# The gate logits as one more column of a projection's weights, in a fused linear-attention kernel

## The chip, the cores and the metric

The kernel runs on one core of one Trainium2 chip. The metric is the device time of one execution in microseconds (us). The kernel before took 189.98 us (median of 3 runs, 189.82 to 190.57).

## The reference

Two linear-attention blocks, A and B, read the same x (2048 rows of 640, bf16), and a gate mixes their outputs:

```
g = sigmoid((x * gate_w).sum(-1))                 # one number per row
block(x, wqkv, wo):                               # 32 heads of 20
    q, k, v = x @ wqkv, by heads
    phi(t) = where(t > 0, t + 1, exp(t)) + 1e-6
    kv = phi(k)^T v;  z = sum of phi(k) over the rows      # per head
    o = (phi(q) kv) / (phi(q) z + 1e-6)
    return o @ wo
out = g * block_A + (1 - g) * block_B
```

## The kernel before, in words

The five engines are TensorE (PE: matmuls, with PEld its weight loads), VectorE (DVE), ScalarE (ACT), GpSimd (POOL) and SyncE (SP, which issues most loads and stores). The order of nearly all work is written out by hand in the program; each engine runs its own instructions in that order and waits where an input isn't ready. PE's results go to PSUM, in four slots of two banks that are used in rotation (`ps`, lines 74 to 81): a slot can be written again when its last reader is done.

x is held twice: `xn` has rows on the partitions (16 chunks of 128 rows), `xT` is transposed (5 column blocks of 128 by 2048 rows). The first four chunks are transposed by PE (`x_transpose`, line 207, a DVE copy out of PSUM at line 214), the other twelve by transposing loads (line 155).

The start (lines 137 to 155): x arrives in four pieces and the k weights of A, `wk[0]`, in five column blocks, on the queues of SP and ACT in turn: SP has x 0, weights 0, weights 2, weights 3 and 4; ACT has x 1, weights 1, x 2, x 3. Then SP issues the q weights of A (line 151) and the fifteen transposing loads. `k_first` (line 265) does the first four chunks of k: transposes of chunks 0 and 1, their matmuls on column blocks 0 and 1, the transpose of chunk 2, and so on, as the pieces arrive. A chunk of k is 10 matmuls (5 column blocks by two halves `hf` of 320 columns; `k_mm`, line 249), and then phi (class `Phi`): ACT takes the exponential `e` (line 225), DVE clamps it (`clamp`, line 230) and takes the larger of it and t + 1 (`top`, line 239) into `pk`.

Then come, for A, the chunks 4 to 15 of k and the first five units of q. `q_pass` (line 743) has the other five q units (`q_unit`: 10 matmuls of 512 columns, and phi), and between the first and the second of them the gate pass and `z_rows` (line 510, the sum of `pk` over the rows, `zA`, which DVE brings to `zr`). `x_sum`, `k_sum` and `sq_sum` are sums on DVE for products done with seven instead of eight multiplications (Strassen); `g_strassen` (line 458) is such a product. In it, `rec_pass` (line 573) computes the denominators of A, `denA`, on PE; DVE multiplies them by a gate factor and takes the reciprocal.

The gate pass (`gate_pass`, line 198): the gate weights came by a load of 640 single elements (line 776, `gcol`), are widened to 32 equal columns by DVE (line 791, `gwr`), and PE multiplies them with `xT` in 40 matmuls (`by_group`, line 188) into `lg`. All 32 partitions of a group hold the same logits, in the layout of the denominators: partition 32 j + h, column for a row of x. ACT takes exp(-logit) and exp(logit) (line 204, `geA` and `geB`), DVE adds 1 (line 205). The denominators of A are multiplied by 1 + exp(-logit) = 1/g, those of B by 1 + exp(logit) = 1/(1 - g), so that the normalization does the gating too (line 582).

After that come the k and q of B in one interleaved stage, its `g` product, the folding of v and wo into one matrix for each block (`M`; for A it goes through `m_rows` in DRAM), and the output products with seven multiplications for a pair of chunks (lines 907 on), each stored by SP.

Of the kernel before, what the change touches and what calls it, by code (L numbers as in the profile page):

```python
# [8 lines left out]
P = 128  # L9
FP32 = mybir.dt.float32  # L10
BF16 = mybir.dt.bfloat16
ACT = mybir.ActivationFunctionType
# [4 lines left out]
DT = D // P  # L17
# [3 lines left out]
HB = 512  # L21
# [11 lines left out]
def kernel(  # L33
# [47 lines left out]
    def ps(name, slot=None):  # L81

        return ps_raw(name, slot).bitcast(FP32).rearrange("p (b n) -> p b n", b=2)
# [16 lines left out]
    ones = persist.tile([P, H], BF16, name="ones")  # L100
    gwr = persist.tile([P, DT, H], BF16, name="gwr")
    hc, ic = ST // 2, 2 * P
# [18 lines left out]
    )]  # L121
    ge = [persist.tile([P, 2 * RB], FP32, name=f"ge{b}") for b in "AB"]

# [10 lines left out]
    wq = [None, None]  # L134
    wk[0] = wpool.tile([P, DT, D], BF16, tag="wk", name="wkA")
    def load_x(eng, lo, hi):
        eng.dma_start(out=xn[:, lo:hi, :], in_=xb0[:, lo:hi, :])

    def load_wk(eng, lo, hi):
        eng.dma_start(out=wk[0][:, lo:hi, :], in_=wq_dram[0][:, lo:hi, D:2 * D])  # L140

# [3 lines left out]
    load_wk(nc.scalar, 1, 2)  # L145
    load_wk(nc.sync, 2, 3)
    load_x(nc.scalar, 2, 3)
    load_wk(nc.sync, 3, DT)
    load_x(nc.scalar, 3, 4)
    wq[0] = wpool.tile([P, DT, D], BF16, tag="wq", name="wqA")  # L150
    nc.sync.dma_start(out=wq[0][:], in_=wq_dram[0][:, :, 0:D])
    gcol = persist.tile([P, DT], BF16, name="gcol")
    for n in range(1, NB):
# [27 lines left out]


    warm = ps("warm", 3)
    one_l, one_r = [nc.const_aps.tensor(1.0, [P, n], BF16) for n in (P, HB)]
# [12 lines left out]

    def gate_pass():

        pt = ps("lg")  # L200
        for h in range(2):
            by_group(pt[:, 0, h * RB:(h + 1) * RB], gwr, xT, h)
        for b in range(2):
            nc.scalar.activation(out=ge[b][:], in_=pt[:, 0, :], func=ACT.Exp, scale=(-1.0, 1.0)[b])
            nc.vector.tensor_scalar(ge[b][:], ge[b][:], 1.0, 1e30, op0=ALU.add, op1=ALU.min)

    def x_transpose(i, slot, eng, cuts=(0, DT)):
        pt = ps_raw("xt", slot)
        for c in range(DT):
            nc.tensor.transpose(out=pt[:, c * P:(c + 1) * P], in_=xn[:, i, c * P:(c + 1) * P], identity=ident[:])  # L210
        copy = nc.scalar.copy if eng == "act" else nc.vector.tensor_copy
        src = pt[:, 0:D].rearrange("p (c n) -> p c n", c=DT)
        for lo, hi in zip(cuts, cuts[1:]):
            copy(out=xT[:, lo:hi, i * P:(i + 1) * P], in_=src[:, lo:hi])

    class Phi:
# [31 lines left out]

    def k_mm(b, i, c, pt, hf):
        nc.tensor.matmul(  # L250
            pt[:, hf, 0:HF], lhsT=xT[:, c, i * P:(i + 1) * P], rhs=wk[b][:, c, hf * HF:(hf + 1) * HF],
            start=(c == 0), stop=(c == DT - 1),
        )

    def k_done(b, i, pt):
        phi(pk[:, i, :].rearrange("p (b n) -> p b n", b=2), pt[:, :, 0:HF])

# [7 lines left out]
    def k_first():  # L265

        pts = [ps("kA", (2 + i) % 4) for i in (0, 1)]

        def part(i, cs):
            for c in cs:  # L270
                for hf in range(2):
                    k_mm(0, i, c, pts[i], hf)

        for i in range(2):
            x_transpose(i, i, "dve", (0, 2, DT))
        for i in range(2):
            part(i, (0, 1))
        x_transpose(2, 0, "dve", (0, 2, DT))
        for i in range(2):
            part(i, (2,))  # L280
        pts.append(ps("kA", 1))
        part(2, (0, 1, 2))
        x_transpose(3, 0, "dve")
        for i in range(3):
            part(i, (3, 4))
            k_done(0, i, pts[i])
        k_chunk(0, 3, 0)

# [284 lines left out]
    def rec_pass(b, zsel, slot):  # L573
# [5 lines left out]
        for h in range(2):  # L579
            part = slice(h * RB, (h + 1) * RB)  # L580
            d1 = work.tile([P, RB], FP32, tag="d1", name="d1")
            nc.vector.scalar_tensor_tensor(
                out=d1[:], in0=pt[:, 0, part], scalar=EPS, in1=ge[b][:, part], op0=ALU.add, op1=ALU.mult
            )
# [158 lines left out]
    def q_pass(units):  # L743

        units = list(units)
        q_unit(0, *units.pop(0))
        gate_pass()
        zr = z_rows(0)
        for k in range(2):
            x_sum(1 + k)  # L750
            q_unit(0, *units.pop(0), True)
# [10 lines left out]
    with tc.manual_schedule():  # L762
# [8 lines left out]
        for i in range(hc, ST - 2):  # L771
            k_chunk(0, i)
            if i == hc:
                sq_sum(4, 0)
    with nc.allow_non_contiguous_dma(reason="640 elements, one to a partition and column"):
        nc.sync.dma_start(out=gcol[:], in_=gate_w.rearrange("(c p) -> p c", p=P))
    for n in range(1, NB):
# [4 lines left out]
    load_wo(0, nc.sync)  # L782
    wk[1] = load_w(1, "k", nc.sync)

# [3 lines left out]
    with tc.manual_schedule():  # L788
        k_chunk(0, ST - 2)
        turn[0] = (turn[0] + 1) % 4  # L790
        nc.vector.tensor_copy(out=gwr[:], in_=gcol[:, :, None].to_broadcast([P, DT, H]))
        k_chunk(0, ST - 1)
        k_sum(0, 1)
        zsel = q_pass([(m, 1) for m in range(DT)])
# [69 lines left out]

        scratch = ctx.enter_context(tc.tile_pool(name="scratch", bufs=1, space=bass.MemoryType.DRAM))
        m_rows = scratch.tile([D, D], BF16, name="m_rows")

# [144 lines left out]
```

## Time and profile before

| | |
|---|---|
| median of 3 runs | 189.98 us |
| the profiled execution's own time | 191.16 us |
| its span (first to last instruction) | 189.4 us |
| PE busy | 184.4 us (97%) |
| DVE busy | 156.0 us (82%) |
| ACT busy | 86.7 us (46%) |
| read from and written to HBM | 10.00 and 3.44 MB |

The busy time of PE counts an instruction from its start to its end, and matmuls overlap, so the distance from one matmul's start to the next one's tells more. "Chain" is the work that ended last, followed back from the last instruction: at each step to what released it. "Landing" is the time from a load's issue to the signal that it is complete. A group of a line is written as: line, engine, operation, output <- inputs, shape.

### The profile page before, as it was taken

To read this page: it belongs to the slowest core of one execution; us is meant where nothing else is said; L and a number is where in the kernel's file an instruction comes from. 1 tells how busy PE (TensorE), PEld (TensorE's weight loads), DVE (VectorE), ACT (ScalarE), POOL (GpSimd) and SP (SyncE) were. 2 spreads that over 40 slices of the span, in tenths; PEclk is the share of its full clock that TensorE was granted. 3 is DMA by queue.
4 is the path that set the end of the run, shared out by engine and by line. 5 is a ranking of instruction groups with operands and counts; after the bars stand their busy time and mean duration, and the time that the engine had idled before them with its cause. 6 is when DMAs were issued, how large, how long until landed. Compare 5 with 4: busy or idle time off the path is not lost.

```text
span 189.4 us, 3688 instructions
## 1 busy us (share of the span) xinstructions
PE 184.4 (97%) x1494; PEld 123.6 (65%) x1494; DVE 156.0 (82%) x267; ACT 86.7 (46%) x134; POOL 8.6 (5%) x23
## 2 busy tenths in 40 slices
PE   8899999999999999999999999999999999999992
PEld 3566657766567677676666665767677776777771
DVE  1368968999898999998898987999997989787553
ACT  2055478544963351563959685662611611111110
POOL 8900000000000000000000000000000000000000
PEclk9999999999999999999999999999999999999999
DMA  6984439992040000005000000146600003213112
GB/s 181 321 147 88 105 61 315 324 194 106 3 143 31 3 0 0 0 3 165 8 3 2 0 0 0 29 137 214 146 0 3 0 3 108 99 39 106 69 69 71
DMA packets 19759, 15.64 MB, mean 83 GB/s; under 512 B 9502, under 2 KB 19614, under 8 KB 19742
## 3 DMA queue, kind: packets, MB, share of 16 engines
q1 hardware_dynamic: 18878, 14.59, 28.0%
q10 hardware_dynamic: 864, 0.82, 1.3%
q8 instruction: 11, 0.18, 0.4%
q14 instruction: 6, 0.05, 0.1%
HBM read 10.00 MB, written 3.44 MB: 71 GB/s over the span
## 4 chain that ended last, share of the span: by engine, by line
PE 91%; DMA 3%; DVE 2%; ACT 1%; ACTq 0%; issue 0%; DVEq 0%
PE gs L453 16%; PE qA L294 11%; PE kA L250 11%; PE kB L250 11%; PE q L348 7%; PE ox L653 6%; PE oy L653 5%; PE oz L653 5%; DMA xn<-in_A_x_dram 3%; PE ow L653 3%; PE gB L424 2%; PE gA L424 2%; PE qB L294 1%; PE q L294 1%; DVE osb L658 1%; PE mA L872 1%
## 5 line engine op out<-in xcount | busy, mean ns | idle before, releaser
L250 PEld LDWEIGHTS <-xT 128*128 128x128 bf16 x320 | 31.4, 99 | 15.0 <-issue 0.2
L230 DVE TENSOR_SCALAR e<-e 128x640 bf16<-128x640 bf16 (+2 forms) x56 | 19.3, 344 | 6.9 <-ACT e L225 6.7
L250 PE MATMUL kB<-wkB,xT 128*128 128x320 bf16 x160 | 24.2, 299 | 0.0
L250 PE MATMUL kA<-wkA,xT 128*128 128x320 bf16 x160 | 23.4, 306 | 0.0
L294 PE MATMUL qA<-xT,wqA 128*128 128x512 bf16 x100 | 22.4, 379 | 0.0
L294 PEld LDWEIGHTS <-wqA 128*128 128x128 bf16 x100 | 11.6, 118 | 9.3 <-issue 0.3
L225 ACT ACTIVATE e<-kA 128x640 bf16<-128x640 f32 x16 | 11.1, 704 | 13.3 <-PE kA L250 13.2
L453 PEld LDWEIGHTS <-xn 128*128 128x128 bf16 x128 | 12.2, 98 | 5.2 <-issue 0.5
L225 ACT ACTIVATE e<-kB 128x640 bf16<-128x640 f32 x16 | 11.3, 708 | 9.0 <-PE kB L250 8.9
L239 DVE SCALAR_TENSOR_TENSOR pk<-kA,e 128x640 bf16<-128x640 f32 x16 | 13.2, 824 | 1.7
L239 DVE SCALAR_TENSOR_TENSOR pk<-kB,e 128x640 bf16<-128x640 f32 x16 | 13.2, 823 | 1.5
L225 ACT ACTIVATE e<-qA 128x1024 bf16<-128x1024 f32 x10 | 10.2, 1024 | 8.6 <-PE qA L294 8.1
L697 ACT COPY u<-ox 128x320 f32<-128x320 f32 x8 | 3.4, 426 | 21.9 <-PE ox L653 21.9
L225 ACT ACTIVATE e<-q 128x512 bf16<-128x512 f32 x18 | 10.8, 598 | 5.4 <-PE q L348 3.8
L653 PEld LDWEIGHTS <-xT 128*128 128x128 bf16 x85 | 8.0, 98 | 3.0 <-DVE xT L592 0.2
L653 PEld LDWEIGHTS <-pqTA 128*128 128x128 bf16 x85 | 7.9, 98 | 2.9 <-issue 0.2
L653 PEld LDWEIGHTS <-pqTB 128*128 128x128 bf16 x80 | 7.8, 98 | 3.0
L453 PE MATMUL gs<-pk,xn 128*128 128x320 bf16 x64 | 9.5, 299 | 0.0
L348 PE MATMUL q<-xT,wqB 128*128 128x512 bf16 x32 | 9.5, 379 | 0.0
L658 DVE TENSOR_TENSOR osb<-oz,u 128x320 bf16<-128x320 f32 (+1 forms) x18 | 8.0, 452 | 1.6 <-PE oz L653 0.9
L424 PEld LDWEIGHTS <-xn 128*128 128x128 bf16 x64 | 6.3, 98 | 3.0 <-issue 0.4
L681 ACT COPY p1s<-ox 128x320 f32<-128x320 f32 x8 | 3.4, 426 | 10.0 <-PE ox L653 10.0
(145 smaller groups left out, 319.5 us busy)
## 6 DMA issues: line engine op xcount, KB each, us to landing
out_dram<-osb SPq DMA_DIRECT2D x14, 160.0 KB, 1.8
xn<-in_A_x_dram SPq DMA_DIRECT2D x3, 640.0 KB, 6.7
wqA<-in_A_wqkv_dram SPq DMA_DIRECT2D x1, 800.0 KB, 6.6
wvA<-in_A_wqkv_dram SPq DMA_DIRECT2D x1, 800.0 KB, 10.3
wkB<-in_B_wqkv_dram SPq DMA_DIRECT2D x1, 800.0 KB
wqB<-in_B_wqkv_dram SPq DMA_DIRECT2D x1, 800.0 KB, 4.5
wvB<-in_B_wqkv_dram SPq DMA_DIRECT2D x1, 800.0 KB, 4.5
MA<-m_rows SPq DMA_DIRECT2D x1, 800.0 KB, 4.5
```

The lines of the kernel that those rows point to most:

```text
L225: nc.scalar.activation(out=to, in_=part, func=ACT.Exp)
L230: nc.vector.tensor_scalar(self.e, self.e, 1.0, EPS, op0=ALU.min, op1=ALU.add)
L239: nc.vector.scalar_tensor_tensor(out=dst, in0=src, scalar=1.0 + EPS, in1=e, op0=ALU.add, op1=ALU.max)
L250: nc.tensor.matmul(pt[:, hf, 0:HF], lhsT=xT[:, c, i * P:(i + 1) * P], rhs=wk[b][:, c, hf * HF:(hf + 1) * HF], start=(c == 0), stop=(c == D ...
L294: nc.tensor.matmul(dst, lhsT=mixed(wq[b][:, c, :], m), rhs=xT[:, c, n * HB:(n + 1) * HB], start=first, stop=last,)
L348: nc.tensor.matmul(dst, lhsT=left(c), rhs=right(c), start=first and k == 0, stop=k == len(cs) - 1, skip_group_check=not first,)
L424: nc.tensor.matmul(pt[:, hf, 0:HF], lhsT=xn[:, i, c * P:(c + 1) * P], rhs=pk[:, i, hf * HF:(hf + 1) * HF], start=(i == 0), stop=(i == ST - 1),
L453: nc.tensor.matmul(pt[:, n, 0:HF], lhsT=left[:, i, n * P:(n + 1) * P], rhs=right[:, i, :], start=(first and i == 0), stop=(i == hc - 1), s ...
L653: nc.tensor.matmul(dst, lhsT=left[:, c, r0:r0 + P], rhs=right[:, c, :], start=(first and c == 0), stop=(c == DT - 1), skip_group_check=not ...
L658: nc.vector.tensor_tensor(out=dst, in0=acc, in1=sb, op=ALU.add)
L681: nc.scalar.copy(out=self.p1s[:], in_=self.at("x"))
L697: nc.scalar.copy(out=self.u2[:], in_=self.at("x"))
```

## The change

The gate logits are no longer a pass of their own. The gate weights become column 640 of the tile of A's k weights, so that the second half of each `kA` matmul has 321 columns and the logit of every row comes out in PSUM column 320 of that half, with rows on the partitions. ACT takes its exponential by chunk (`gl`, one column each); after the last chunk DVE makes both factors from it (`gate_rows`: a clamp, a reciprocal, an added 1). `gate_spread` brings them into the layout of the denominators: one transpose on PE (fp32, with an fp32 identity that POOL makes, held in the not yet used `GT[0]`), a copy by ACT, a store of 32 rows to DRAM (`g_rows`), and four loads that broadcast them over 32 partitions each into `ge`.

The column itself comes from a load of the gate weights as 5 rows of 128 (`g5`), transposed by PE and copied by DVE (`gate_column`), early in `k_first`. There the order is now: transposes of chunks 0 and 1, first halves of chunk 0 (two matmuls), `gate_column`, first halves of chunk 1, second halves of both, column block 2 of both, transposes of chunks 2 and 3, then the rest. Each `x_transpose` is copied by DVE (blocks 0 and 1) and ACT (blocks 2 to 4). The loads: SP has x 0, weights 0, gate weights, x 2 and 3 in one; ACT has x 1, weights 1, weights 2, weights 3 and 4. The load of B's k weights is issued a little later in program order.

```diff
-    wk[0] = wpool.tile([P, DT, D], BF16, tag="wk", name="wkA")
+    wk[0] = wpool.tile([P, DT, D + 2], BF16, tag="wk", name="wkA")
...
     load_x(nc.sync, 0, 1)
     load_x(nc.scalar, 1, 2)
     load_wk(nc.sync, 0, 1)
     load_wk(nc.scalar, 1, 2)
-    load_wk(nc.sync, 2, 3)
-    load_x(nc.scalar, 2, 3)
-    load_wk(nc.sync, 3, DT)
-    load_x(nc.scalar, 3, 4)
+    nc.sync.dma_start(out=g5[:], in_=gate_w.rearrange("(c p) -> c p", p=P))
+    load_wk(nc.scalar, 2, 3)
+    load_x(nc.sync, 2, 4)
+    load_wk(nc.scalar, 3, DT)
...
-    def gate_pass():
-        pt = ps("lg")
-        for h in range(2):
-            by_group(pt[:, 0, h * RB:(h + 1) * RB], gwr, xT, h)
-        for b in range(2):
-            nc.scalar.activation(out=ge[b][:], in_=pt[:, 0, :], func=ACT.Exp, scale=(-1.0, 1.0)[b])
-            nc.vector.tensor_scalar(ge[b][:], ge[b][:], 1.0, 1e30, op0=ALU.add, op1=ALU.min)
+    def gate_column(pt):
+        nc.tensor.transpose(out=pt[:, 2 * HB:2 * HB + DT], in_=g5[:], identity=ident[0:DT, 0:DT])
+        nc.vector.tensor_copy(out=wk[0][:, :, D:D + 1], in_=pt[:, 2 * HB:2 * HB + DT, None])
+    def gate_rows():
+        nc.vector.tensor_scalar(gf[:, 1], gl[:], 1e-30, 1e30, op0=ALU.max, op1=ALU.min)
+        nc.vector.reciprocal(out=gf[:, 0], in_=gf[:, 1])
+        nc.vector.tensor_scalar(gf[:], gf[:], 1.0, 1e30, op0=ALU.add, op1=ALU.min)
+    def gate_spread():
+        pt = ps("gt")
+        nc.tensor.transpose(out=pt[0:2 * ST, 0, 0:P], in_=gf[:].rearrange("p b i -> p (b i)"), identity=ident32)
+        rows = work.tile([2 * ST, P], FP32, tag="d1", name="gr")
+        nc.scalar.copy(out=rows[:], in_=pt[0:2 * ST, 0, 0:P])
+        nc.sync.dma_start(out=g_rows[:], in_=rows[:])
+        by_group = g_rows[:].rearrange("(g j r) p -> j g (r p)", g=4, j=4)
+        for j in range(4):
+            nc.sync.dma_start(
+                out=ge[32 * j:32 * j + 32].rearrange("p b (h n) -> p (b h) n", h=2),
+                in_=by_group[j][None].to_broadcast([H, 4, RB]),
+            )
...
     def k_mm(b, i, c, pt, hf):
+        n = HF + (b == 0 and hf == 1)
         nc.tensor.matmul(
-            pt[:, hf, 0:HF], lhsT=xT[:, c, i * P:(i + 1) * P], rhs=wk[b][:, c, hf * HF:(hf + 1) * HF],
+            pt[:, hf, 0:n], lhsT=xT[:, c, i * P:(i + 1) * P], rhs=wk[b][:, c, hf * HF:hf * HF + n],
...
     def k_done(b, i, pt):
-        phi(pk[:, i, :].rearrange("p (b n) -> p b n", b=2), pt[:, :, 0:HF])
+        f = Phi(pk[:, i, :].rearrange("p (b n) -> p b n", b=2), pt[:, :, 0:HF])
+        if b == 0:
+            nc.scalar.activation(out=gl[:, i:i + 1], in_=pt[:, 1, HF:HF + 1], func=ACT.Exp)
+        f.clamp()
+        f.top()
...
-        for i in range(2):
-            x_transpose(i, i, "dve", (0, 2, DT))
-        for i in range(2):
-            part(i, (0, 1))
-        x_transpose(2, 0, "dve", (0, 2, DT))
+        pt = [x_transpose(i, i) for i in range(2)]
+        part(0, (0, 1), (0,))
+        gate_column(pt[0])
+        part(1, (0, 1), (0,))
+        for i in range(2):
+            part(i, (0, 1), (1,))
         for i in range(2):
             part(i, (2,))
-        pts.append(ps("kA", 1))
+        for i in (2, 3):
+            x_transpose(i, i - 2)
+        pts.append(ps("kA", 0))
         part(2, (0, 1, 2))
-        x_transpose(3, 0, "dve")
         for i in range(3):
             part(i, (3, 4))
             k_done(0, i, pts[i])
-        k_chunk(0, 3, 0)
+        k_chunk(0, 3, 1)
...
         q_unit(0, *units.pop(0))
-        gate_pass()
         zr = z_rows(0)
+        gate_spread()
...
-    wk[1] = load_w(1, "k", nc.sync)
...
-        nc.vector.tensor_copy(out=gwr[:], in_=gcol[:, :, None].to_broadcast([P, DT, H]))
         k_chunk(0, ST - 1)
+        gate_rows()
+        wk[1] = load_w(1, "k", nc.sync)
```

## The prediction

> **What bounds the kernel now.** I read the busy times first, then the chain of work that ended last in order of time, then the instructions in order of time for the two stretches that the change touches. The page's first line:
>
> ```profile
> PE 184.4 (97%) x1494; PEld 123.6 (65%) x1494; DVE 156.0 (82%) x267; ACT 86.7 (46%) x134; POOL 8.6 (5%) x23
> ```
>
> TensorE (PE) has almost no idle time. The chain (start, length, what) says where it has some, and what the gate costs:
>
> ```profile
> 1.73 5.91 DMA xn<-in_A_x_dram
> 7.64 0.05 issue
> 7.69 0.45 PE xt L210 x5
> ...
> 39.87 2.16 PE qA L294 x10
> 42.03 1.21 PE lg L193 x39
> 43.24 1.09 PE zA L516 x32
> 44.32 4.45 PE qA L294 x20
> ```
>
> To 7.64 us a load of x is waited for; from there to 115 us the chain is PE work with no gap. PE's time there counts in full, and the gate logits (`lg`) stand in the chain with 1.21 us. The only other gap is 3.4 us around 115 to 118.4, where PE waits for the last results of its own work; it moves with PE. What could keep PE from using a gain is VectorE (DVE), so I read its instructions around the gate pass:
>
> ```profile
> 41.11 0.82 DVE L239 SCALAR_TENSOR_TENSOR pk<-kA,e 128x640 bf16<-128x640 f32 x1
> 41.85 1.48 DVE L592 TENSOR_TENSOR pqTB<-pk 128x2560 bf16<-128x2560 bf16 x1
> 43.25 0.42 DVE L230 TENSOR_SCALAR e<-e 128x1024 bf16<-128x1024 bf16 x1
> 43.77 1.23 DVE L239 SCALAR_TENSOR_TENSOR pqTA<-qA,e 128x1024 bf16<-128x1024 f32 x1
> 44.91 0.42 DVE L205 TENSOR_SCALAR geA<-geA 128x512 f32<-128x512 f32 x1
> 45.24 0.42 DVE L205 TENSOR_SCALAR geB<-geB 128x512 f32<-128x512 f32 x1
> 45.58 0.82 DVE L521 TENSOR_TENSOR zr<-zA,E 128x640 bf16<-128x640 f32 x1
> ...
> 59.95 0.69 DVE L325 TENSOR_TENSOR SQ<-xT,SQ 128x1024 bf16<-128x1024 bf16 x1
> 61.06 0.42 DVE L582 SCALAR_TENSOR_TENSOR d<-denA,geA 128x256 f32<-128x256 f32 x1 [0.42 <-PE denA L193]
> ```
>
> DVE runs nearly without a pause, but its last step here (line 582) still waits 0.42 us for PE. In the stretch 45.6 to 65.4 the table by stretches gives DVE 18.20 busy of 19.80 us. So it has 1.6 us to give, if it isn't itself made late.
>
> **The change, part by part.**
>
> *Gate pass out of PE:* -1.21 us (the chain's row). The first `q` unit's matmuls end at 42.03; `zA` then starts there instead of at 43.24. Its first matmuls read old chunks of `pk`, and the last chunk is written at 41.11 + 0.82 = 41.93, so nothing is late.
>
> *The logits' new place:* 80 matmuls of `kA` with 321 columns for 320. Matmuls of 320 columns start 0.136 us apart and of 512 columns 0.216, so a column is 0.4 ns: 80 x 0.4 ns = +0.03 us. Every width in this trace is even; what an odd one does isn't shown. The bounds are nothing and the pitch that the same matmuls have before 6.85 us, 0.267 us, which would be +10.5 us; I take the slope, to which all rows keep.
>
> *16 small Exp on ACT:* ACT takes 704 ns for 640 columns and 1024 ns for 1024, so about 0.17 us with one column, 2.7 us in all. ACT idles 0.65 us ahead of nearly each `e` of the `kA` chunks; that covers it. DVE's step waits for `e`, which comes first. Without the cover it would be 0.17 us a chunk.
>
> *Transpose of the factors on PE, fp32, behind `zA`:* bf16 transposes of x start 0.056 us apart. The trace has no fp32 one: at least 0.06 us, at most four times that for the load of the weights and the pass (0.099 us is a weight load of 128 columns), 0.06 x 4 + 0.1 = 0.36 us. I take +0.2 us, the middle. It doesn't wait: its input is ready near 42.6 us, PE is there at 43.1.
>
> *DVE at the gate:* two steps of line 205 go (44.91 to 45.58, 0.67 us) and the copy into `gwr` (0.31 us, in time where DVE would wait for `e` anyway). Three dependent small steps come in ahead of the `k_sum` at 41.85. A TENSOR_SCALAR takes 320 ns for 640 columns and 424 for 1024, so 0.15 us for none; RECIPROCAL takes 1753 ns for 256 columns, so 0.11 us more for 16; dependent steps stand 0.1 us apart (43.67 to 43.77). That is about 0.68 us. Bounds: 3 x 0.06 (the smallest MEMSET, 59 ns) = 0.2, and 2.2 us if the reciprocal's time were fixed. So `zr` starts where it did, while what lies between is 0.68 us later. That matters once: the third `q` unit of this pass writes the PSUM slot of the first, which DVE frees at 45.00, then at 45.68. PE would be there at 42.03 + 1.09 + 0.2 + 2.17 = 45.49. So PE may wait 0.2 us; with the low bound not at all. I take +0.1 us. From `zr` on DVE has 14.3 us of work to the end of line 325's sums, so it is done near 60.0; `denA` would end near 60.1. Line 582 still waits for PE, and the gain goes through to the rest.
>
> *Store by rows, four broadcast loads:* SP is idle here (it waits 12.9 us for `qA` before it issues `wqB` at 53.31). A store to `m_rows` lands after 2.0 us, 800 KB from there after 4.5; with five issues of 0.4 us the factors are in place near 52.5 us, and line 582 reads them at 60. Free; if not, `rec_pass` would wait. The later issue of `wkB`, the missing `gcol` load (0.58 us of SP at 25.67) and a second identity on POOL, which is done at 9.9 us, are free in the same way.
>
> *The start.* Before, the third piece of x (third on ACT's queue) landed at 7.64, and 32 matmuls and 10 transposes behind it led to the first `qA` matmul at 12.62. On SP's queue the third load landed at 1.71 + 4.4 = 6.11; the trace's completion signals put the fourth ones at 8.57 (SP, 800 KB then through) and 8.79 (ACT, 640 KB). PE is slow there too: `kA` matmuls start 0.267 us apart until 6.85 and 0.136 after. Now both late pieces of x are one load in SP's fourth place, and the weights' third piece and last two pieces are third and fourth on ACT. Four things can be last:
> - PE itself: twelve matmuls and one small transpose from 5.01 on (eight slow, four fast) end near 7.5; then 10 transposes x 0.056, of which the first five, a copy and its signals take 0.83 (as from 7.69 to 8.525 before), and 28 matmuls x 0.136 = 3.81: 7.5 + 0.83 + 3.81 = 12.2.
> - x: 640 KB of SP's queue, halfway between 6.11 and 8.57: 7.34, and + 4.64 = 12.0.
> - weights 2: between 6.11 and 7.64 (the third places); four matmuls more, + 5.18: 11.3 to 12.8.
> - weights 3 and 4: 800 KB on ACT's queue: between 8.79 and 8.79 + 1.15 (the step from 7.64 to 8.79 once more) = 9.94; 22 matmuls follow, + 2.99: 11.8 to 12.9.
>
> So the first `qA` comes between 12.2 and 12.9. The last item, in its middle, gives 12.35; I take 12.4, **-0.2 us**, bounds -0.4 and +0.3. The gate column's own load is 1.2 KB; if it landed as late as the third SP load (6.11), PE would lose 0.6 us of its slack and come to 12.8, inside the bounds.
>
> The Trainium skill (DMA: Bandwidth & Descriptors, Rules for kernel authors) says that spreading loads over the issuing engines brings no bandwidth, since all queues run on the same 16 DMA engines and interleave. The trace agrees so far that both queues' last loads landed 0.2 us apart. By it the bytes would land as before, the last at 8.79, the start would be PE's 12.2, and the sum 0.2 us lower; an estimate.
>
> **Sum:** -1.21 + 0.03 + 0.2 + 0.1 - 0.2 = **-1.08 us**. The profiled execution took 191.16 us (span 189.4), which makes 190.08; the median of the runs shown is 189.98, 1.18 below the profiled one, and the difference taken from it gives **188.9 us** (-0.57%). A measurement tells about 0.5%, 0.95 us, from no change: 189.03 and 190.93 are the borders.
>
> **Rivals.**
> - *DVE becomes the bound at the gate.* The three small steps delay the PSUM slot. With the upper bound of 2.2 us the slot is free at 47.2, PE waits 1.7 us, and the sum is -1.08 - 0.1 + 1.7 = +0.5: 190.5; with 1.5 us it is 189.8. For it: DVE has no pause from 41.1 to 46.3. Against: RECIPROCAL has 256 columns in its row, here it has 16. Chance 0.10.
> - *The start is late.* ACT's last weights share the DMA engines with `wqA`, which SP issues at 4.06 and which landed at 10.66. If they land only then, the first `qA` is at 13.65, +1.03: -0.88 + 1.03 = +0.15, 190.1. For it: ACT's third load landed 1.5 us behind SP's third. Chance 0.13.
> - *Slower: the column waits for all weights.* The gate column is written into the tile that the weight loads still fill. If DVE's copy has to wait for the last of them (8.8 to 9.9), then eight matmuls (1.1), ten transposes and their copy (0.83 from the first) and 28 matmuls (3.81) stand behind it: 14.5 to 15.6, +1.9 to +3.0, less 0.88: about 191.5. It decides from a column at 7.8 us on. For it: PE stands in order behind that copy. Against: line 214 copied into `xT` at 4.67 while loads into other columns of `xT` were under way from 4.48 on. Chance 0.09.
> - *Odd widths.* From 14 ns a matmul on (80 x 14 ns = 1.1 us) nothing of the gain is left; 26 ns (2.1 us) gives 190.9, and the slow pitch of 0.267 us some 199. Nothing in the trace speaks for it. Chance 0.08.
>
> **How the numbers follow.** Forecast 0.60, from 188.5 (all low ends: -1.52) to 189.7 (all high ends, with 0.2 at the slot: -0.3); about 0.43 of it lies under 189.03. Same takes 0.17 of it, 0.09 of DVE and the late start's 0.13: 0.39. Slower: the column, odd widths and 0.01 of DVE: 0.18. The range goes from 188.2 (a DVE that gives back its idle time) to 190.4, with the late start and most of DVE's rival in it, and leaves out the two slower ones.
>
> **What would show it.** Right: no `lg`; `zA` directly behind `qA`; `kA` matmuls 0.136 us apart; the first `qA` near 12.4; line 582's step waiting for PE and not for `ge`; from there on all one us earlier. Wrong: a gap on PE ahead of the third `q` unit (DVE), ahead of the second halves of the first `kA` chunks (the column), or ahead of their columns 3 and 4 (the weights); a `kA` pitch of 0.150 us or more.

## The result and the profile after

The changed kernel takes 190.56 us (median of 22 runs, 190.18 to 191.16), the kernel before 190.12 us on the same chip (22 runs, 189.60 to 190.64). The ratio is 1.0028, with a 95% interval of 1.0017 to 1.0039: 0.44 us slower, which is less than the 0.5% that was to count as a change. A gain of 1.08 us had been forecast. The profiled execution of the changed kernel took 190.57 us with a span of 188.9 us. The median of the kernel before is 0.14 us above the one shown ahead of the prediction, and its profiled execution, 191.16 us, is 1.04 us above that.

The first line of the page of the changed kernel:

```profile
PE 182.9 (97%) x1447; PEld 122.4 (65%) x1456; DVE 154.6 (82%) x265; ACT 88.5 (47%) x153; POOL 9.1 (5%) x25
```

PE is busy 1.5 us less than before, in a span that is 0.5 us shorter than that of the profiled execution before. The chain of work that ended last, in its two stretches (start, length, what):

```profile
1.73 5.52 DMA wkA<-in_A_wqkv_dram
7.25 0.04 issue
7.29 0.71 PE kA L274 x4
8.00 0.29 PE xt L233 x5
8.29 0.02 issue
8.31 0.30 DVE xT L236
8.62 0.02 issue
8.64 0.49 ACT xT L236
9.13 0.04 issue
9.17 4.00 PE kA L274 x28
...
38.36 0.84 DVE pk L262
39.19 0.04 issue
39.23 1.52 PE kA L274 x10
...
42.92 1.20 PE zA L546 x32
44.12 0.21 PE gt L219
44.33 1.73 PE qA L324 x8
```

The row of `lg` is gone, and in its place stands `gt`, the fp32 transpose, with 0.21 us: the gate part of the change does what was forecast. But two things are new in the chain. At the start it is the third piece of the weights that is waited for, and then two copies out of PSUM, one after the other, ahead of 28 matmuls. At 38 us, where PE had no gap before, it waits for DVE (`pk`, line 262).

What can be counted from every profile is when chunk 2 is first transposed by PE, when the first `qA` matmul starts, and what is left from there to the end. The column behind that is the median of the runs less that rest: an estimate of where the first `qA` stands in a middling execution, if the rest is the same in every execution (in two profiles of before it is 178.54 and 178.56, see e8). The kernels ran on several chips, and the median of before differs between these (190.12 beside the changed kernel, 190.25 beside e1 to e8, 190.27 beside e9 to e12, 190.49 beside e13 to e16). So the last column compares with before on the same chip: its median there less 178.54. In e13, e14 and e16 one or two of the 12 executions ran slower as a whole at a granted clock of 0.99, and the last two columns leave these out. All in us:

| kernel | chunk 2's transposes | first `qA` | distance | own time less first `qA` | median less that | later than before, same chip |
|---|---|---|---|---|---|---|
| before | 7.69 | 12.62 | 4.93 | 178.54 | 11.58 | 0 |
| after | 7.84 | 13.00 | 5.16 | 177.57 | 12.99 | +1.41 |
| e1, start only | 7.42 | 12.57 | 5.15 | 178.58 | 12.90 | +1.19 |
| e2, gate only | 7.29 | 12.35 | 5.06 | 177.62 | 12.32 | +0.61 |
| e3, one exponential | 7.73 | 12.91 | 5.18 | 177.41 | 12.86 | +1.15 |
| e4, rows later | 7.60 | 12.78 | 5.18 | 177.79 | 12.80 | +1.09 |
| e5, two memsets | 7.32 | 12.50 | 5.18 | 177.13 | 12.89 | +1.18 |
| e6, other slot | 7.98 | 12.94 | 4.96 | 177.57 | 12.74 | +1.03 |
| e7, gate best | 6.89 | 11.84 | 4.95 | 177.07 | 12.31 | +0.60 |
| e8, before again | 6.37 | 11.30 | 4.93 | 178.56 | 11.58 | -0.13 |
| e9, loads of before | 7.30 | 12.47 | 5.17 | 177.62 | 12.31 | +0.58 |
| e10, order of before | 7.52 | 12.48 | 4.96 | 177.54 | 12.56 | +0.83 |
| e11, stretch filled | 7.62 | 12.58 | 4.96 | 177.03 | 12.94 | +1.21 |
| e12, before, one memset | 7.09 | 12.03 | 4.94 | 178.89 | 11.51 | -0.22 |
| e13, before, five loads | 7.28 | 12.21 | 4.93 | 177.90 | 11.98 | +0.03 |
| e14, column late | 6.53 | 12.38 | 5.85 | 177.04 | 13.09 | +1.14 |
| e15, after, five loads | 8.17 | 13.35 | 5.18 | 177.84 | 13.07 | +1.12 |
| e16, column apart | 7.90 | 14.01 | 6.11 | 177.08 | 13.19 | +1.24 |

The change gains 0.97 us behind the first `qA` (178.54 to 177.57) and loses 1.41 us ahead of it (11.58 to 12.99): +0.44 us, as measured. How far the last column can be trusted is seen from kernels that share a start: those with the start of before (e8, e12, e13) lie between -0.22 and +0.03, and those with the start of the changed kernel (e3, e4, e5, e15) between +1.09 and +1.18, where the changed kernel itself has +1.41. Differences under about 0.3 us in it mean nothing.

### The profile page after: what moved, and what is told of

Its sections match the earlier page's. It is cut to its first block, busy times and chain, and to the rows that moved or that the text cites. A ratio compares the mean times of both kernels' runs of the same rounds, so it can differ in the third digit from the quotient of the medians.

```text
span 188.9 us, 3632 instructions
## 1 busy us (share of the span) xinstructions
PE 182.9 (97%) x1447; PEld 122.4 (65%) x1456; DVE 154.6 (82%) x265; ACT 88.5 (47%) x153; POOL 9.1 (5%) x25
## 4 chain that ended last, share of the span: by engine, by line
PE 90%; DVE 3%; DMA 3%; ACT 1%; issue 1%; ACTq 0%; DVEq 0%
PE gs L483 16%; PE qA L324 11%; PE kB L274 11%; PE kA L274 11%; PE q L378 7%; PE ox L683 6%; PE oy L683 5%; PE oz L683 5%; DMA wkA<-in_A_wqkv_dram 3%; PE ow L683 3%; PE gB L454 2%; PE gA L454 2%; PE qB L324 1%; PE q L324 1%; DVE osb L688 1%; PE mA L898 1%
## 5 line engine op out<-in xcount | busy, mean ns | idle before, releaser
L274 PE MATMUL kA<-wkA,xT 128*128 128x320 bf16 (+1 forms) x160 | 23.0, 299 | 1.6 <-ACT xT L236 0.6
L483 PEld LDWEIGHTS <-xn 128*128 128x128 bf16 x128 | 12.2, 98 | 5.2 <-issue 0.5
```

The costliest lines, as they stand in the source:

```text
L274: nc.tensor.matmul(pt[:, hf, 0:n], lhsT=xT[:, c, i * P:(i + 1) * P], rhs=wk[b][:, c, hf * HF:hf * HF + n], start=(c == 0), stop=(c == DT - 1),
L483: nc.tensor.matmul(pt[:, n, 0:HF], lhsT=left[:, i, n * P:(n + 1) * P], rhs=right[:, i, :], start=(first and i == 0), stop=(i == hc - 1), s ...
```

## The experiments

A kernel called e1 to e16 is compared with runs of the kernel before on its own chip; ratios have their 95% interval.

### The two halves of the change alone

e1 has the loads, copies and order of the changed kernel in the kernel before, with the old gate; e2 has the gate of the changed kernel with the start of before, its 1.2 KB load on POOL's queue. The code shown here and below is cut to the lines that matter.

```diff
 e1, on before (k_first and x_transpose are those of after too, without gate_column):
-    load_wk(nc.sync, 2, 3)
-    load_x(nc.scalar, 2, 3)
-    load_wk(nc.sync, 3, DT)
-    load_x(nc.scalar, 3, 4)
+    nc.sync.dma_start(out=g5[:], in_=gate_w.rearrange("(c p) -> c p", p=P))
+    load_wk(nc.scalar, 2, 3)
+    load_x(nc.sync, 2, 4)
+    load_wk(nc.scalar, 3, DT)
 e2, on after (loads, k_first and x_transpose are those of before); against before's k_first:
-            part(i, (0, 1))
+            part(i, (0, 1), (0,))
+        gate_column(pt[0])
+        for i in range(2):
+            part(i, (0, 1), (1,))
```

> The kernel before with only the start of the changed one: its order of the loads (the gate weights' 5 rows are loaded too and not used), its split of the transposes' copies over DVE and ACT, and its order of the first four chunks of k; the old gate pass stays. Theory S (the start eats the gain: chunk 2 of k reuses the PSUM slot of its own transposes, which is free only when ACT has copied behind DVE, and the third weights come late): first qA matmul at 12.9 to 13.2 us, time 0.4 to 0.8 us over before. Rival D (the start costs nothing, DVE's sixteen longer waits in the k stage eat it): within 0.1 us of before.

> The changed kernel with the start of before: its loads, its copies by DVE alone, its order of the first chunks, with the gate column put in between the first and the second halves of chunks 0 and 1; the gate weights are loaded on POOL's queue. Theory S: 0.6 to 0.9 us under before, since PE has 1.0 us less and only the small waits of DVE remain. Rival D: within 0.2 us of before, since the sixteen Exp and what waits for them are all there.

e1: 191.48 us, ratio 1.0061 (1.0037 to 1.0085). e2: 189.94 us, ratio 0.9974 (0.9955 to 0.9993). The start alone loses about 1.2 us, more than the 0.4 to 0.8 expected; the gate alone gains about 0.5, a little less than the 0.6 to 0.9 expected. In the table, e1's first `qA` stands 1.19 us later than that of before, with no gate column in it. That is as much as in the other kernels with the changed start (1.09 to 1.41), so the changed start costs this much even without the column. PE's instructions in e1 (what ended the idle time ahead of a group stands in brackets):

```profile
7.42 0.73 PE L211 MATMUL xt<-ident,xn 128*128 128x128 bf16 x10 [0.37 <-DMA xn<-in_A_x_dram]
8.77 3.96 PE L251 MATMUL kA<-wkA,xT 128*128 128x320 bf16 x28 [0.61 <-ACT xT L214]
```

Chunk 2's first matmul comes 1.35 us after its first transpose; before it is 0.83. In the start of before the column has a price of its own: e2 stands 0.61 us later than before.

### Is the profiled execution of before typical?

> The kernel before once more, for a second profile. The profiled execution of before took 191.16 us, 1 us over the median of its runs. If the late piece of x there (7.64 us) is what made that one slow, this profile shows an earlier landing and a first qA matmul near 11.7 us wherever its time is near 190.1; if it is something else, the first qA matmul stays at 12.6.

e8 is the kernel before once more: 190.14 us, ratio 1.0004 (0.9979 to 1.0029). Its profiled execution took 189.86 us, and its chain has the same load as before with another length:

```profile
1.73 4.59 DMA xn<-in_A_x_dram
6.32 0.05 issue
6.37 0.45 PE xt L210 x5
```

x's third piece landed at 6.32 us, not at 7.64. From chunk 2's first transpose to the first `qA` both profiles have 4.93 us, and from there to the end 178.54 and 178.56. So in these two the time of before is x's landing and a constant, and the profile that the prediction was built on was one with a late landing: by the median, its first `qA` came 1.04 us later than in a middling one.

### Which part of the new start

e9 gives the changed kernel the loads of before (`g5` on POOL's queue), e10 the order and the DVE copies of before, e6 another PSUM slot: chunk 2's matmuls go to a slot other than that of its own transposes, and the transposes of chunk 3 move behind the first six of them.

```diff
 e6, on after:
-        for i in (2, 3):
-            x_transpose(i, i - 2)
-        pts.append(ps("kA", 0))
+        x_transpose(2, 0)
+        pts.append(ps("kA", 1))
         part(2, (0, 1, 2))
+        x_transpose(3, 0)
...
-        k_chunk(0, 3, 1)
+        k_chunk(0, 3, 0)
```

> The changed kernel with the transposes of chunk 3 behind chunk 2's first six matmuls, so that chunk 2's k is written into slot 1 and doesn't wait for both copies of its own transposes. Theory S: PE's gap of 0.6 us ahead of chunk 2 goes, first qA matmul 0.4 to 0.6 us earlier, time 0.4 to 0.6 us under the changed kernel. Rival L (the loads set the start: the weights' blocks 3 and 4 are last): less than 0.2 us under it.

> The changed kernel with the loads of before in their old order (the gate weights on POOL's queue); its order of the first k, its split copies and all else stay. In the second profile of before, x 2 landed at 6.3 us and the first qA matmul came at 11.3; in the changed kernel at 13.0. Theory O (the order and the slot: both pieces of x, and all column blocks up to 2, are wanted before the fourth chunk's work can fill in): the first qA stays at 12.6 or later, time within 0.3 us of the changed kernel. Rival L (the loads): 0.6 us or more under the changed kernel.

> The changed kernel with its loads, but the order of the first k and the copies by DVE alone as in before (the gate column between first and second halves). Theory O: 0.6 us or more under the changed kernel. Rival L: within 0.3 us of it, the first qA at 12.6 or later, with PE waiting for x 2 and 3 ahead of the transposes.

e6: 190.31 us, 1.0001 (0.9986 to 1.0016). e9: 189.93, 0.9978 (0.9961 to 0.9995). e10: 190.10, 0.9979 (0.9963 to 0.9996). Each takes something back, and none gets to the start of before: the first `qA` stands 1.03, 0.58 and 0.83 us later than there. PE in e6:

```profile
7.98 0.45 PE L233 MATMUL xt<-ident,xn 128*128 128x128 bf16 x5 [0.24 <-DMA xn<-in_A_x_dram]
8.82 1.00 PE L274 MATMUL kA<-wkA,xT 128*128 128x320 bf16 x6 [0.39 <-DVE xT L236]
```

Chunk 2's first matmul follows its first transpose by 0.84 us, where the changed kernel has 1.33 (7.84 to 9.17): the wait for ACT's copy is gone, so it came from the shared slot. Chunk 3's transposes now take their 0.28 us behind that matmul, so the distance to the first `qA` falls by 0.2 us only, to 4.96. By its ratio e6 is about 0.5 us under the changed kernel (the two intervals make that 0.2 to 0.9), as expected, but its trace accounts for 0.2 us of that alone, and there the transposes came late (7.98, where PE waited 0.24 us for x).

e9 and e10 are both about 0.5% under the changed kernel, so each of the two theories, order and loads, got the sign that it asked for. Loads and order aren't two costs to be added: with either of them put back the start is at +0.58 or +0.83, with both (e2) at +0.61, no better than with the loads alone. What then stays, 0.6 us, is the column. It doesn't add to the rest either, since e1 has +1.19 without it. The new loads alone and the new order alone, without the column, weren't run.

### The column at the start

e7 is e2 with the two memsets of e5 (below), and with the factors' DVE steps behind the first `q` unit's phi and `gate_spread` behind the third `q` unit. e11 is e7 with the third column block taken into the stretch that covers the column. e14 is e7 with no column in chunks 0 and 1 (`k_mm` and `k_done` leave it out there, not shown), e16 is e14 with those two chunks' logits as ten one-column matmuls.

```diff
 e7, on e2:
         k_chunk(0, ST - 1)
-        gate_rows()
...
         q_unit(0, *units.pop(0))
+        gate_rows()
         zr = z_rows(0)
-        gate_spread()
         for k in range(2):
             x_sum(1 + k)
             q_unit(0, *units.pop(0), True)
+        gate_spread()
 e11, on e7:
-            part(i, (0, 1), (0,))
+            part(i, (0, 1, 2), (0,))
...
-            part(i, (2,))
+            part(i, (2,), (1,))
 e14, on e7:
-            part(i, (0, 1), (0,))
-        gate_column(pt[0])
...
-            part(i, (0, 1), (1,))
-        x_transpose(2, 0, "dve", (0, 2, DT))
+            part(i, (0, 1))
+        gate_column(x_transpose(2, 0, "dve", (0, 2, DT)))
 e16, on e14:
             part(i, (3, 4))
+            for c in range(DT if i < 2 else 0):
+                nc.tensor.matmul(pts[i][:, 1, HF:HF + 1], lhsT=xT[:, c, i * P:(i + 1) * P],
+                    rhs=wk[0][:, c, D:D + 1], start=(c == 0), stop=(c == DT - 1))
```

> The gate-only kernel (start of before, gate as a column) with the two MEMSETs and with the factors made behind the first q unit's phi and transposed on PE behind the third q unit. If theory P holds and the slot wait at the third q unit is the other loss, PE keeps 0.9 to 1.0 us of the gate pass: 0.5 to 0.7 us under the gate-only kernel, 1.0 to 1.3 us under before. If not: as the gate-only kernel, 0.5 us under before.

> The gate-best kernel, with two more first-half matmuls ahead of the gate column in chunks 0 and 1, so that PE has work while the column's load and copy are under way (it lost 0.27 and 0.45 us there in the gate-only kernel). If PE's waits there set the start: 0.3 to 0.5 us under the gate-best kernel. If x 2 sets it anyway: the same within 0.2.

> The version e7 with no logits column in the matmuls of chunks 0 and 1 (the logits of those two chunks are left out, their exponentials set to 1), and the gate weights turned behind the transposes of chunk 2. Theory: what the start of e7 still has over that of the kernel before is the wait for the column's copy ahead of the second half of chunks 0 and 1 (the rows showed 0.27 and 0.45 us); without it, the first qA starts about 0.7 us sooner than in e7, near 11.6, and the time is near 188.7 (ratio to before 0.992). Rival: those two waits only bring forward a later wait for x or for the weights; then the time stays within 0.2 us of e7's 189.4.

> The version e14 with the logits of chunks 0 and 1 computed after all: five one-column matmuls behind the last pieces of each of the two chunks, ten in all. By the 5-by-5 transpose's row (0.17 us alone) and the pitch of the 128-column transposes (0.09 or less) they should take 0.3 to 0.9 us, part of it beside waits. Theory: 0.2 to 0.6 us over e14, so 188.9 to 189.3, at or a little under e7. Rival: they cost as much as the wait that they avoid, and the time is e7's 189.4 or above.

e7: 189.38 us, 0.9950 (0.9932 to 0.9968), faster than both kernels: 0.56 us under e2, as expected, and 0.87 under before, where 1.0 to 1.3 was expected. e11: 189.97, 0.9988 (0.9959 to 1.0016). e14: 190.15, 0.9967 (0.9949 to 0.9986). e16: 190.41, 0.9997 (0.9967 to 1.0027). PE in e7, where the small transpose turns the gate weights:

```profile
4.99 0.98 PE L277 MATMUL kA<-wkA,xT 128*128 128x320 bf16 x4
5.90 0.17 PE L209 MATMUL xt<-ident,g 5*128 5x5 bf16 x1
6.35 0.71 PE L277 MATMUL kA<-wkA,xT 128*128 128x321 bf16 x4 [0.27 <-DVE wkA L210]
6.89 0.44 PE L235 MATMUL xt<-ident,xn 128*128 128x128 bf16 x5
```

PE doesn't wait for x at 6.89, since x had landed at 6.57; it comes there late, after the wait for DVE's copy of the column. An early landing like that of e8 (6.32) would be of no use to it. e14 was to show the start without that wait, near 11.6 and 188.7 us, and it didn't: by its time and by its ratio it is no faster than e7. PE in e14:

```profile
6.53 0.45 PE L236 MATMUL xt<-ident,xn 128*128 128x128 bf16 x5 [0.35 <-DMA xn<-in_A_x_dram]
7.63 0.16 PE L210 MATMUL xt<-ident,g 5*128 5x5 bf16 x1 [0.65 <-DVE xT L240]
```

Chunk 2 has its turn at 6.53, when x has landed, as in before, but the small transpose goes to the slot of the x transposes and must wait 0.65 us until DVE has copied these out. The distance is 5.85 instead of 4.95: my edit moved the wait, so it doesn't decide what the start would be without the column. e16 tells one price all the same: its distance is 6.11, so ten one-column matmuls cost 0.26 us more. e11 filled the stretch, and 0.3 to 0.5 us under e7 was expected; it is no faster than e7 by its ratio, and its first `qA` stands 1.21 us later than before's. Where the column would cost nothing was not found.

### The gap ahead of chunk 15

The instructions of DVE in the changed kernel:

```profile
35.10 0.32 DVE L253 TENSOR_SCALAR e<-e 128x640 bf16<-128x640 bf16 x1
35.97 0.82 DVE L262 SCALAR_TENSOR_TENSOR pk<-kA,e 128x640 bf16<-128x640 f32 x1 [0.55 <-ACT gl L282]
36.72 0.32 DVE L253 TENSOR_SCALAR e<-e 128x640 bf16<-128x640 bf16 x1
```

One `top` starts 0.46 us late, and the profile blames ACT's small exponential `gl`, which had ended at 35.67. DVE then works without a pause at 1.19 us a chunk while PE needs 1.36, and is still late for chunk 15. Chunk 15 writes the slot of chunk 12 (one slot is skipped in the rotation), not that of 11, so DVE has hardly any slack there. In the kernel before, the `top` of chunk 12 and the first `qA` matmul behind chunk 15 are:

```profile
37.39 0.82 DVE L239 SCALAR_TENSOR_TENSOR pk<-kA,e 128x640 bf16<-128x640 f32 x1
39.71 2.32 PE L294 MATMUL qA<-xT,wqA 128*128 128x512 bf16 x10
```

The `top` ends at 38.21, and chunk 15 starts ten matmuls of 0.136 us ahead of 39.71, at 38.35. In the changed kernel PE follows 0.04 us behind the `top` that it waits for (39.19), so the slack is 0.1 us. Three kernels ask whose stop this is: e3 takes the exponential only for the last chunk (so the logits of the others are left out, POOL sets them to 1), e5 puts two one-column memsets more on DVE at the start, and e12 puts one on DVE in the kernel before, which has no column.

```diff
 e3, on after:
-        if b == 0:
+        if b == 0 and i == ST - 1:
 e5, on after:
-    nc.vector.memset(lift[:], 1.0 + EPS)
+    for _ in range(3):
+        nc.vector.memset(lift[:], 1.0 + EPS)
 e12, on before:
-    nc.vector.memset(lift[:], 1.0 + EPS)
+    for _ in range(2):
+        nc.vector.memset(lift[:], 1.0 + EPS)
```

> The changed kernel with the Exp of the logits' column left out for all chunks but the last; the other logits are replaced by zeros, so the gate is left out for them. Theory S: DVE saves 0.03 us a chunk and at most one stall, 0.2 to 0.5 us under the changed kernel, still not under before by more than 0.1. Rival D: 0.8 us or more under the changed kernel, so clearly under before.

> The changed kernel with two more one-column MEMSETs on DVE at its very start. In the changed kernel and in the three runs that have its gate, DVE stands still for 0.46 us ahead of the 64th instruction of its trace, whichever chunk of k that is and whenever it comes (34.1 to 36.0 us). Theory P (the stop belongs to the place in DVE's instruction stream): with two instructions more it falls behind a step of 0.82 us that covers it, as in the kernel before; PE's gap ahead of chunk 15 shrinks from 0.45 to 0.1 us or less, time 0.3 us under the changed kernel. Rival W (the stop is the longer wait for ACT's Exp of the column, or a load in flight): the stop stays with its chunk, time as the changed kernel.

> The kernel before with one more one-column MEMSET on DVE at its start. Theory P (a stop at the 64th instruction of DVE's trace): that instruction is then the long step of chunk 9, behind a semaphore wait, and DVE stands still for 0.46 us ahead of it, with no gate column in the kernel; DVE has about 0.3 us to spare at chunk 15, so PE loses 0.1 to 0.2 us there and the time rises by as much. If the stop needs the gate's waits: no stop, and the time of before.

e3: 190.27 us, 0.9996 (0.9975 to 1.0016). e5: 190.02, 0.9995 (0.9978 to 1.0012). e12: 190.40, 0.9997 (0.9980 to 1.0014). By the times alone e3 and e5 stand at the edge of what they can tell, and e12 shows nothing; the traces say it plainly. e3, with no exponentials there, has the stop in the same place:

```profile
34.96 0.32 DVE L254 TENSOR_SCALAR e<-e 128x640 bf16<-128x640 bf16 x1
35.80 0.82 DVE L263 SCALAR_TENSOR_TENSOR pk<-kA,e 128x640 bf16<-128x640 f32 x1 [0.52 <-DVE e L254]
```

And e5, with two instructions more on DVE, has none there:

```profile
34.60 0.32 DVE L254 TENSOR_SCALAR e<-e 128x640 bf16<-128x640 bf16 x1
35.05 0.83 DVE L263 SCALAR_TENSOR_TENSOR pk<-kA,e 128x640 bf16<-128x640 f32 x1
```

The kernel before gets the stop from one memset (e12):

```profile
32.89 0.32 DVE L231 TENSOR_SCALAR e<-e 128x640 bf16<-128x640 bf16 x1
33.73 0.82 DVE L240 SCALAR_TENSOR_TENSOR pk<-kA,e 128x640 bf16<-128x640 f32 x1 [0.52 <-DVE e L231]
```

In all of the kernels with the stop (after, e2, e3, e4, e6, e9, e10, e12, e15) the late instruction is the 64th of DVE's records, its semaphore waits counted. There it is a `top`, which has to wait for the clamp ahead of it, and DVE stops 0.46 us. In the other nine the 64th is a clamp right behind a longer step (a `top` in before and e5, a sum in e7), and nothing is seen. So it isn't the gate's exponential. The rest behind the first `qA` is 0.44 us shorter in e5 than in after and 0.34 us longer in e12 than in before: that is the price, in e12 the stop less the slack of 0.1 us. What happens at that instruction isn't shown. The Trainium skill (Runtime: NRT & Kernel Launch, Instruction fetch mechanics) has instructions streamed in blocks, the cost of a crossing mostly hidden; the trace of the changed kernel has instruction loads at 37.9 (16 KB), 38.5 and 38.7 us (8 KB each), but 1.9 us and more behind the stop, and that of e5, which has no stop, has three such loads too (37.7 to 38.2 us), so no tie is shown.

### The gate's steps on DVE

```diff
 e4, on after:
         k_chunk(0, ST - 1)
-        gate_rows()
...
         q_unit(0, *units.pop(0))
+        gate_rows()
         zr = z_rows(0)
-        gate_spread()
         for k in range(2):
             x_sum(1 + k)
             q_unit(0, *units.pop(0), True)
+            if k == 0:
+                gate_spread()
```

> The changed kernel with DVE's three small factor steps moved behind the first q unit's phi, and their transpose on PE behind the second q unit. The third q unit no longer waits for its PSUM slot: 0.1 to 0.2 us under the changed kernel by both theories; 0.5 us or more if DVE's delay there is what eats the gain.

e4: 190.59 us, 1.0023 (1.0006 to 1.0040): no gain over the changed kernel. The 0.19 us that PE waits for the slot of the third `q` unit goes, and in its place PE waits 0.21 us for the input of `gt` (DVE's last step, line 214):

```profile
46.38 0.27 PE L219 MATMUL gt<-GT,gf 128*32 128x128 f32 x1 [0.21 <-DVE gf L214]
```

e7, which puts `gate_spread` one unit further, has neither of the two waits.

### The end

No step of the change was meant to touch the end, yet 0.69 us of its gain lie behind the last matmul's start: 3.74 us to the end of the span before, 3.05 after. There SP waits for the DMA semaphores one after another, in one order. When each wait ended, in us after the last matmul's start, from the records of the traces (the last store landed 2.20 to 2.22 in all four):

| kernel | 1st | 2nd | 3rd | 4th | 5th | last store is in |
|---|---|---|---|---|---|---|
| before | 2.25 | 2.72 | 2.81 | 2.88 | 2.94 | the 1st |
| after | 1.03 | 1.10 | 1.21 | 1.75 | 2.26 | the 5th |
| e13 | 1.03 | 1.10 | 1.26 | 1.78 | 2.25 | the 5th |
| e15 | 2.26 | 2.33 | 2.39 | 2.46 | 2.52 | the 1st |

Eight semaphores are handed to the DMAs in rotation, and the change has four DMAs more (gate load moved, two x pieces merged into one, a store and four loads added). e13 and e15 add four DMAs to before and to after, far from the end: B's k weights in five loads.

```diff
 e13, on before, and e15, on after:
-    wk[1] = load_w(1, "k", nc.sync)
+    wk[1] = wpool.tile([P, DT, D], BF16, tag="wk", name="wkB")
+    for c in range(DT):
+        nc.sync.dma_start(out=wk[1][:, c:c + 1, :], in_=wq_dram[1][:, c:c + 1, D:2 * D])
```

> The kernel before, with B's k weights loaded in five pieces instead of one: four DMAs more, issued at chunk 15 of the k stage, far ahead of their use. Theory: the 0.69 us that the changed kernel gained behind its last matmul comes from which of the eight DMA semaphores its last store has, since SP passes them one after another in a fixed order at the end; four DMAs more move the last store from the first of them to the fifth. From the last matmul's start to the end of the span then 3.05 us instead of 3.74, and the time is 0.65 to 0.7 us below the kernel before (ratio 0.9965). Rival: the gain belongs to something of the gate's (its rows, its store); then 3.74 stays and the time is that of the kernel before within 0.1 us.

> The changed kernel with B's k weights loaded in five pieces instead of one, four DMAs more. Theory of the semaphore of the last store: four DMAs more of a rotation of eight bring it back to the first that SP passes, so the end is again 3.74 us behind the last matmul's start, and the time is 0.65 to 0.7 us over the changed kernel (ratio to before 1.006). Rival: 3.05 stays and the time is that of the changed kernel within 0.1 us (ratio 1.003).

e13: 190.00 us, 0.9964 (0.9945 to 0.9983), and 3.03 us behind the last matmul: as expected, so this gain needs nothing of the gate. e15: 190.91, 1.0019 (1.0001 to 1.0037), and 3.31 us: behind the last matmul the sign is as expected, the size isn't. By its time, where a ratio of 1.006 was expected, nothing is seen against the changed kernel (1.0028): the 0.26 us at the end are no more than the scatter of the start (+1.12 for +1.41 in the table). Its four waits behind the store's cost 0.26 us, 0.065 each. The other 0.43 us are a stop of SP between the first and the second wait, which before has (2.25 to 2.72) and e15 hasn't, though what that wait waits for had landed at 1.21 in both. It is as long as DVE's stop, and SP has ten instructions more in e15. The trace has a load of 8 KB of instructions 0.63 us behind the stop's end in before (189.04 us), and the last one in e15 is at 179.55; that would fit a stop tied to a place in SP's instructions, but it is no more than a fit.

## Why the prediction was wrong

The forecast was faster by 1.08 us, and the kernel is slower by 0.44. Step by step, with what was measured in its place:

| step | predicted, us | measured, us |
|---|---|---|
| gate pass out of PE | -1.21 | -1.10 (`lg`, start to start) |
| 321 columns | +0.03 | +0.05 (`kA` behind the start: 16.35 without the gap, before 16.30) |
| fp32 transpose | +0.2 | +0.13 (`zA` to the next `qA` 1.32, before 1.19) |
| DVE at the gate, third `q` unit's slot | +0.1 | +0.19 |
| small Exp on ACT, DVE in the k stage | 0 | +0.45 (gap ahead of chunk 15) |
| the start | -0.2 | +1.41 |
| the end | not in the sum | -0.69 |
| sum | -1.08 | +0.44 |

The first and the third row are counted from one matmul's start to the next one's, since rows counted so add up. The lines are, before and after:

```profile
41.96 1.28 PE L193 MATMUL lg<-xT,gwr 128*32 128x256 bf16 x40
43.06 1.26 PE L516 MATMUL zA<-pk,ones 128*32 128x320 bf16 x32
44.26 4.51 PE L294 MATMUL qA<-xT,wqA 128*128 128x512 bf16 x20
...
42.85 1.27 PE L546 MATMUL zA<-pk,ones 128*32 128x320 bf16 x32
44.05 0.28 PE L219 MATMUL gt<-GT,gf 128*32 128x128 f32 x1
44.17 4.67 PE L324 MATMUL qA<-xT,wqA 128*128 128x512 bf16 x19
```

**The start failed**, in two ways. The first was in the base. The start was costed against the profiled execution of before, with its first `qA` at 12.62, and the difference was then applied to a median 1.18 us below that execution. The text saw that distance and didn't ask where it lay. It lay in the very stretch that was being costed: x's landing at 7.64, which e8 shows at 6.32. "I take 12.4, -0.2 us" should have been 12.4 against 11.58, +0.8. That alone takes the sum from -1.08 to about -0.06.

The second was in the forecast itself: 12.99 instead of 12.4. The landings weren't at fault: both late pieces of x came at 7.71 (predicted 7.34), weights 2 at 7.25 (6.11 to 7.64), weights 3 and 4 at 8.48, earlier than bounded (8.79 to 9.94). What failed was the item "weights 2 ... four matmuls more, + 5.18": from 7.25 that makes 12.43, and it was 13.00. Its 0.83 us from the first transposes to chunk 2's first matmul measured 1.33 (7.84 to 9.17). They were taken from the old order, where both copies are DVE's and the matmul goes to another slot. In the new order chunk 2's matmuls write the slot of its own transposes, and that slot is free only when ACT's copy is done. The chain shows DVE's copy from 8.31 and ACT's from 8.64, one after the other although they read different columns of the tile, and the matmul at 9.17. With another slot it is 0.84 (e6). Why the two copies didn't run side by side isn't shown.

The Trainium skill's rule that spreading loads brings no bandwidth (DMA: Bandwidth & Descriptors, Rules for kernel authors) was weighed with the last landing at 8.79 and a start of 12.2. The runs don't speak against it, with that landing at 8.48; the start missed 12.2 by PE's waits for weights 2 (chunk 2's transposes at 7.84, not near 7.5) and, above all, for the copies.

**The k stage** was costed at nothing because "ACT idles 0.65 us", and ACT's cover did hold (e3). What the step missed was DVE: its slack at chunk 15 is 0.1 us, by the skipped slot, and a stop of 0.46 us, which nothing in the page of before showed, came to a place where it is seen. The exponential's own part is small: a chunk costs DVE 1.19 us instead of 1.16 in steady work.

**The gate** was right in mechanism and nearly in size: `lg` out and the transpose in make -0.97 us, where -1.01 was forecast. The three steps on DVE, and what the slot waits for:

```profile
42.73 0.17 DVE L212 TENSOR_SCALAR gf<-gl 128x16 f32<-128x16 f32 x1
42.93 0.25 DVE L213 RECIPROCAL gf<-gf 128x16 f32<-128x16 f32 x1
43.22 0.18 DVE L214 TENSOR_SCALAR gf<-gf 128x32 f32<-128x32 f32 x1
43.31 1.49 DVE L622 TENSOR_TENSOR pqTB<-pk 128x2560 bf16<-128x2560 bf16 x1
44.72 0.42 DVE L253 TENSOR_SCALAR e<-e 128x1024 bf16<-128x1024 bf16 x1
45.24 1.23 DVE L262 SCALAR_TENSOR_TENSOR pqTA<-qA,e 128x1024 bf16<-128x1024 f32 x1
```

0.58 us from 42.73 to 43.31, where 0.68 was estimated; the first unit's slot is free at 46.47 and PE goes on at 46.52. PE's wait of 0.19 us is at the upper end of what was allowed for it. DVE gave its delay back by the time it mattered, and the factors through DRAM were not late: line 612 (582 before) still waits for PE.

```profile
61.13 0.42 DVE L612 SCALAR_TENSOR_TENSOR d<-denA,ge 128x256 f32<-128x256 f32 x1 [0.42 <-PE denA L200]
```

**The rivals.** The late start is the nearest, but its price (190.1, +0.15 us) is a third of the loss, and its mechanism isn't what happened: the last weights landed at 8.48, far ahead of `wqA`'s 10.54. The others fell: DVE at the gate (0.19 us of waiting, where its price was 1.7), the column that waits for all weights (DVE copied it at 5.76, while weights 2 landed at 7.25 and weights 3 and 4 at 8.48) and odd widths (+0.05). None of the rivals had the stop of DVE or the end. The 0.69 us at the end are luck: the prediction didn't look there, and without them the kernel would be slower by 1.1 us. With 190.56 us the time is slightly above the range's upper end of 190.4, on the other side of no change than forecast.

Open stay: what stops DVE at its 64th record and SP at the end, why a piece of x lands at 6.3 us in one execution and at 7.6 in another, how the loss at the start divides between loads and order, and how early the first `qA` could be with the column in place.

## What to carry to other kernels

Before a change's difference is applied to a median, find where the profiled execution and the median part, above all in the stretch that the change touches: a second profile of the same kernel would have shown 1.3 us there. When an order is moved, take no interval from the old order for the new one without asking for each buffer who reads it last. And where an engine has a tenth of a microsecond of slack, as DVE at chunk 15, count it as a place where any shift of instructions can come out, and price the end of the kernel apart from its work.

## What was not expected of the hardware

DVE stopped 0.46 us at the 64th of its recorded instructions in each of the nine kernels where that was a step that waits for the one ahead of it. The store's landing at the end was the same in all kernels (2.20 to 2.22 us after the last matmul's start), and yet the span behind it differed by up to 0.69 us with the number of DMAs in the whole kernel. The same load of 160 KB, issued at 1.73 us, landed at 6.32 in one execution and at 7.64 in another, while the one beside it on the other queue landed at 5.83 and 6.11; over the ten kernels that have this load it landed between 5.62 (e11) and 7.85 (e16).
